# Plain 16-bit transposes of the attention outputs, and another table of scheduling settings

## The chip, the cores and the metric

The kernel runs on one core of a Trainium2 chip. The metric is the device time of one execution in microseconds (us). The engines are called by their short names: PE is the matrix engine, DVE the vector engine, ACT the activation engine, POOL the general engine, and SP the engine that issues most of the DMAs.

## The reference

Two attentions over the same x are mixed by a gate. S is 2048 tokens, D is 640, and there are 32 heads of 20.

```python
x = A_x
g = sigmoid((x * gate_w).sum(-1, keepdims=True))
a = full softmax attention: softmax(q k^T * 20**-0.5) v, 32 heads, then @ A_wo
b = sliding attention over 8 keys per query, 2 tokens apart (masked below 0), then @ B_wo
return g * a + (1 - g) * b
```

The full attention has 32 heads x 2048 x 2048 scores. Their exponentials are the bulk of the work.

## The kernel before

**Units and tiles.** The scores of four heads and 512 queries form a group: there are 32 groups (`NG`), 8 sets of heads for each of 4 chunks of queries. A group is cut into 64 units: 128 keys x 512 queries of one head, and so 2048 units in all. One unit is one 512-column matmul of `qk` (line 1515) into one bank of the PSUM. A tile is what one ACT instruction works on: two or three units side by side in one of two score buffers of 1536 columns (`exp`, line 1538, writes `ebuf`).

**Units that go to DVE.** The third bank of a score buffer can hold instead a unit that "rides" on the tile: DVE makes 16-bit integers of it, which read as bf16 are an approximate exponential (line 1528, `uD`). For each four such units (a quad) DVE also makes three shifted copies (line 797, `eD`), and POOL scales a copy of v for these (line 789, `vS`). PE then adds `uD` and the three `eD` to the output with one matmul each. So a unit is worth one ACT share of a tile, or one `uD`, three quarters of an `eD`, and four matmuls in place of one.

**PV and norm.** `pv` (line 1583) accumulates v^T p of a whole group in one bank, `obank`. When a group is done, `gen_norm` moves it out: DVE transposes it in blocks of 32 x 32 (line 758, `oTt`), takes reciprocals (line 762), POOL multiplies by gate and reciprocal (lines 764 and 770; DVE for the last group), and DVE transposes the bf16 result back (line 772, `oN1`). In the kernel before, line 770 writes the tokens in an order such that the back-transpose can take two bf16 as one 32-bit element: 256 elements in place of 512. Tokens then lie interleaved in `oN1` and `oTd`, and `paired` gives every later matmul a strided view of them, 32 columns at a time (lines 557 and 1063).

**Side work.** Generators with priorities do the rest in the gaps: projections of q, k and v, the sliding attention (`gen_b`, `gen_bproj`), the output projection of a finished chunk (`gen_fold`), and for the last chunk all of that projection but its last head set (`gen_prefold`, `gen_prefold2`). `tail` adds that last set (line 1063), adds up (lines 1076, 1082, 1085), and sends the last four row blocks off, two by ACT's DMA queue and two by SP's (line 1090). Matmuls of `filler` (line 1604) have no use but to keep PE busy where it would wait.

**What sets the order.** `_Sched` has an assumed time for every operation and lays the program out one tile after the other. Eighteen settings steer the choices: how far ahead of PE a side operation may be placed, which priorities get a third bank, how idle DVE must be for a riding unit (`DWAIT`, `DIDLE`, `DIDLE2`), the load under which fillers are put in (`FILL`), and so on. `PLAN` is a table of them by tile number: at tile s the row of s, if there is one, replaces all eighteen.

Of the kernel before, what the change touches and what calls it, by code (L numbers as in the profile page):

```python
# [5 lines left out]
FP32 = mybir.dt.float32  # L6
# [44 lines left out]
    0: ((0.34, 0.64), 0.37, 6.3, 2.5, 0.51, -1.0, -0.1, 11.8, 4.5, 7.2, 0.52, 0.47, 4.4, 1.86, 0.0, 0.85, 2, 0.0),  # L51
    10: ((0.34, 0.64), 0.37, 6.3, 2.5, -0.17, -1.0, -0.1, 13.02, 4.5, 7.2, 0.52, 0.47, 4.4, 1.86, 0.0, 0.85, 2, 0.0),
    20: ((0.34, 0.64), 0.21, 6.3, 6.6, -0.17, -1.0, -0.1, 13.02, 4.5, 8.28, 0.52, 0.47, 4.4, 1.86, 0.0, 0.85, 2, 0.0),
    30: ((0.28, 0.52), 0.35, 2.5, 6.6, 0.49, -1.55, -0.55, 9.24, 6.7, 7.2, 0.53, 0.57, 4.23, 4.64, 0.02, 0.85, 2, 1),
    50: ((0.28, 0.52), 0.35, 2.5, 6.6, 0.49, -1.55, -0.55, 9.24, 6.7, 7.2, 0.25, 0.57, 4.23, 4.64, -0.13, 0.85, 2, 1),
    60: ((0.28, 0.52), 0.35, 2.5, 6.6, 0.49, -1.55, -0.55, 9.24, 6.7, 7.2, 0.53, 0.57, 4.23, 4.28, 0.16, 0.85, 2, 1),
    70: ((0.28, 0.52), 0.1, 2.5, 6.6, 0.49, 0.2, -0.55, 9.24, 6.7, 7.2, 0.5, 0.57, 4.23, 4.64, 0.02, 0.85, 2, 1),
    80: ((0.28, 0.52), 0.34, 2.5, 5.5, 0.49, -1.55, -0.62, 9.24, 7.0, 7.2, 0.53, 0.57, 4.55, 4.64, 0.02, 0.85, 2, 1),
    90: ((0.28, 0.52), 0.3, 2.5, 6.6, 0.49, -1.55, -0.55, 9.24, 6.7, 7.8, 0.5, 0.57, 4.23, 4.64, 0.02, 0.85, 2, 1),
    110: ((0.28, 0.52), 0.3, 2.5, 6.6, 0.49, -1.55, -0.55, 8.84, 6.7, 7.8, 0.5, 0.57, 4.23, 4.64, 0.02, 0.85, 2, 0),  # L60
    120: ((0.28, 0.52), 0.3, 5.5, 6.6, 0.49, -1.34, -0.55, 8.84, 6.7, 7.8, 0.5, 0.57, 4.23, 4.64, 0.05, 0.85, 2, 0),
    130: ((0.28, 0.52), 0.19, 5.5, 6.3, 0.49, -0.24, -0.53, 9.24, 6.7, 11.3, 0.53, 0.57, 4.23, 4.93, -0.13, 0.89, 2, -3),
    140: ((0.28, 0.52), 0.3, 2.5, 2.5, 0.87, -1.55, -0.55, 8.84, 6.7, 7.8, 0.5, 0.57, 3.8, 4.64, 0.02, 0.85, 2, 0),
    170: ((0.28, 0.52), 0.3, 2.5, 2.5, 0.87, -1.28, -0.55, 8.42, 6.7, 7.8, 0.5, 0.54, 3.8, 4.64, 0.02, 0.85, 2, 0),
    180: ((0.28, 0.52), 0.39, 6.6, 2.5, 0.87, -1.55, -0.65, 10.03, 6.7, 7.8, 0.5, 0.57, 3.8, 3.83, 0.02, 0.87, 2, -3),
    190: ((0.28, 0.52), 0.19, 2.5, 2.5, 0.7, -1.55, -0.55, 7.32, 6.7, 7.8, 0.5, 0.5, 3.8, 2.96, 0.02, 0.85, 2, -3),
    200: ((0.23, 0.54), 0.35, 2.5, 2.5, 0.87, -1.55, -0.55, 7.13, 6.7, 7.71, 0.5, 0.57, 3.46, 4.13, 0.02, 0.86, 2, -3),
    210: ((0.28, 0.52), 0.3, 2.5, 2.5, 0.9, -1.55, -0.6, 7.13, 6.7, 7.71, 0.5, 0.49, 3.46, 4.64, 0.02, 0.85, 2, -3),
    220: ((0.32, 0.54), 0.3, 2.5, 2.5, 1.16, -1.55, -0.6, 7.13, 6.7, 7.71, 0.5, 0.49, 3.46, 4.64, 0.02, 0.85, 2, -3),
    230: ((0.28, 0.52), 0.3, 2.5, 2.5, 0.9, -1.55, -0.6, 7.61, 6.7, 7.71, 0.5, 0.49, 3.46, 4.64, 0.02, 0.81, 2, -3),  # L70
    250: ((0.28, 0.52), 0.3, 2.5, 2.5, 0.9, -1.48, -0.27, 7.13, 4.5, 7.32, 0.5, 0.36, 3.46, 4.64, 0.02, 0.66, 2, -3),
    280: ((0.28, 0.52), 0.3, 2.5, 2.5, 0.9, -1.48, -0.27, 7.13, 4.5, 7.32, 0.5, 0.41, 3.46, 4.64, 0.02, 0.66, 2, -3),
    290: ((0.28, 0.52), 0.3, 2.5, 5.5, 0.9, -1.6, -0.6, 7.13, 6.7, 10.69, 0.5, 0.49, 3, 4.64, 0.02, 0.67, 2, -3),
    310: ((0.28, 0.52), 0.3, 2.5, 5.5, 0.9, -1.6, -0.6, 14.73, 6.7, 10.69, 0.5, 0.49, 5.63, 4.64, 0.02, 0.67, 2, -3),
    320: ((0.28, 0.52), 0.3, 2.5, 5.5, 1.26, -1.56, -0.6, 7.13, 6.7, 10.69, 0.5, 0.53, 3, 4.64, 0.02, 0.67, 2, -3),
    330: ((0.27, 0.53), 0.26, 2.5, 5.5, 0.58, -1.6, -0.6, 7.13, 4.5, 10.54, 0.5, 0.49, 3, 4.64, 0.11, 0.67, 2, -3),
    340: ((0.27, 0.53), 0.3, 2.5, 5.5, 0.9, -1.5, -0.6, 7.13, 7.0, 10.54, 0.41, 0.49, 3.17, 4.64, 0.2, 0.67, 2, -3),
    350: ((0.27, 0.53), 0.26, 1.0, 5.5, 0.58, -1.6, -0.6, 7.13, 4.5, 10.54, 0.5, 0.49, 3, 4.64, 0.02, 0.69, 1, -3),
    360: ((0.28, 0.52), 0.37, 2.5, 5.5, 1.26, -1.56, -0.6, 7.13, 6.7, 10.69, 0.5, 0.53, 5.91, 4.64, 0.02, 0.67, 2, -3),
    400: ((0.28, 0.52), 0.37, 2.5, 5.5, 1.26, -1.56, -0.6, 7.13, 4.5, 10.69, 0.5, 0.53, 5.91, 4.64, 0.02, 0.67, 2, -3),  # L80
    410: ((0.23, 0.54), 0.22, 2.5, 6.3, 1.26, -1.56, -0.6, 7.13, 6.7, 10.69, 0.5, 0.53, 5.35, 4.64, 0.02, 0.6, 2, -3),
    420: ((0.24, 0.49), 0.3, 2.5, 5.5, 1.26, -1.56, -0.59, 7.13, 6.7, 10.69, 0.5, 0.53, 6.0, 4.64, 0.02, 0.67, 2, -3),
    430: ((0.24, 0.49), 0.3, 2.5, 5.5, 1.26, -1.56, -0.59, 7.13, 6.7, 10.69, 0.51, 0.53, 6.0, 4.64, 0.02, 0.67, 2, -3),
    450: ((0.26, 0.56), 0.3, 2.5, 5.5, 1.26, -1.56, -0.59, 7.13, 6.7, 10.69, 0.5, 0.53, 6.0, 4.64, 0.02, 0.67, 2, 0),
    480: ((0.26, 0.56), 0.3, 2.5, 5.5, 1.26, -1.4, -0.59, 9.8, 6.7, 10.69, 0.5, 0.53, 6.0, 4.64, 0.02, 0.67, 2, 0),
    500: ((0.26, 0.56), 0.3, 2.5, 5.5, 1.26, -1.56, -0.59, 7.13, 6.7, 10.69, 0.5, 0.53, 6.0, 4.64, 0.02, 0.76, 2, -1.5),
    510: ((0.26, 0.56), 0.3, 2.5, 5.5, 1.26, -1.56, -0.09, 7.13, 6.7, 10.69, 0.5, 0.53, 6.0, 4.64, 0.02, 0.76, 2, -3),
    530: ((0.21, 0.59), 0.3, 2.5, 6.6, 1.26, -1.56, -0.43, 7.13, 6.7, 10.69, 0.5, 0.53, 6.0, 4.64, -0.23, 0.76, 2, -3),
    540: ((0.21, 0.58), 0.3, 6.6, 5.5, 1.26, -0.43, -0.09, 7.13, 6.7, 10.33, 0.5, 0.53, 6.0, 4.64, 0.08, 0.76, 2, -3),
    550: ((0.21, 0.59), 0.3, 2.5, 6.6, 1.26, -1.56, -0.43, 7.13, 6.7, 11.31, 0.49, 0.53, 6.0, 4.64, -0.36, 0.76, 2, -3),  # L90
    570: ((0.2, 0.61), 0.3, 2.5, 6.6, 1.26, -1.56, -0.43, 7.13, 6.7, 10.69, 0.5, 0.53, 6.0, 4.64, -0.23, 0.76, 2, -3),
    580: ((0.2, 0.56), 0.3, 2.5, 5.5, 1.26, -1.56, 0.15, 9.66, 6.7, 8.54, 0.49, 0.48, 6.0, 4.64, -0.36, 0.76, 2, -3),
    590: ((0.2, 0.56), 0.26, 2.5, 1.0, 1.26, -1.56, 0.15, 7.13, 6.7, 11.31, 0.49, 0.31, 6.0, 4.64, -0.36, 0.76, 2, -3),
    600: ((0.28, 0.45), 0.32, 2.5, 5.5, 1.26, -0.49, -0.43, 10.79, 5.5, 10.35, 0.57, 0.53, 6.0, 4.64, -0.33, 0.66, 2, -3),
    630: ((0.28, 0.45), 0.32, 2.5, 5.5, 0.96, -0.49, -0.43, 10.79, 5.5, 10.35, 0.65, 0.53, 6.0, 4.64, -0.33, 0.66, 2, -3),
    660: ((0.28, 0.45), 0.32, 2.5, 5.5, 0.96, -0.1, -0.27, 10.79, 5.5, 10.35, 0.65, 0.53, 6.0, 4.64, -0.33, 0.66, 2, -3),
    670: ((0.28, 0.5), 0.32, 2.5, 5.5, 1.11, -0.49, -0.43, 10.79, 6.2, 10.35, 0.65, 0.55, 6.5, 4.81, -0.39, 0.62, 2, -3),
    690: ((0.3, 0.64), 0.32, 2.5, 2.5, 0.49, -1.0, -0.1, 11.8, 5.5, 7.2, 0.52, 0.47, 4.4, 4.0, 0.0, 0.85, 2, 0.0),
    700: ((0.42, 0.48), 0.32, 6.3, 5.5, 0.76, -0.49, -0.43, 10.79, 5.5, 10.35, 0.65, 0.53, 6.0, 4.64, -0.33, 0.63, 2, -3),
# [220 lines left out]
def _build(ctx, nc, A_x, A_wqkv, A_wo, B_wqkv, B_wo, gate_w, out):  # L320
# [221 lines left out]
    def mm_group(b, mms, reads, cost, first=True, last=True, per=1):  # L542
# [3 lines left out]
        for i0 in range(0, n, per):  # L546
            i1 = min(n, i0 + per)
            yield ("pe", sum(cost[i0:i1]) if isinstance(cost, list) else cost * (i1 - i0), rdy)

            def fn(e, i0=i0, i1=i1):  # L550
                ins = None
                for i in range(i0, i1):
                    o, l, r = mms[i]
                    n_ = P if callable(l) else l.shape[-1]
                    for j in range(0, n_, 32):
                        k = min(j + 32, n_)
                        ins = e.matmul(o[j:k, :], l(j) if callable(l) else l[:, j:k], r, start=(first and i == 0),  # L557
                                       stop=(last and i == n - 1), skip_group_check=True)
                return ins

            c = sum(cost[i0:i1]) if isinstance(cost, list) else cost * (i1 - i0)
            if i0 == 0 and first:
                T("pe", c, fn, reads=reads, writes=[("side", b)], mode="col")
            else:
                T("pe", c, fn, reads=reads, accum=[("side", b)], mode="col")
# [190 lines left out]
    def gen_norm(g):  # L756
# [9 lines left out]

        ib = _ap(rcp, 0, [[4, 4], [2, 2], [1, 2], [0, 32]])
        oo = _ap(oN[0], 0, [[128, 4], [1, 2], [64, 2], [2, 32]])
        ii = _ap(oTt, 0, [[128, 4], [64, 2], [32, 2], [1, 32]])
# [1008 lines left out]
```

## Time and profile before

| What | Value |
|---|---|
| Median of three runs (lowest to highest) | 837.19 us (836.29 to 837.24) |
| The profiled execution: its own time | 837.19 us |
| The profiled execution: its span | 835.4 us |
| Granted PE clock, mean | 0.998 |
| Busy time in the span: PE, ACT, DVE, POOL | 789.3, 803.9, 683.7, 138.7 us |
| ACT tiles of 1024, 1536 and 512 columns | 479, 255, 1 |
| Riding units (`uD`), shifted copies (`eD`) | 324, 243 |

The span is the time from the first to the last instruction in the trace. The execution's own time is 1.8 us longer, and equals the median. Busy times are those of a single execution. A "wait" in the profile is idle time of an engine before an instruction, with what ended it.

### The profile page before, as it was taken

The numbers are of one execution on the slowest core, as the hardware profiler recorded it, in microseconds if no ns is written. First come the engines' busy times: TensorE is split into PE (matmuls) and PEld (weight loads), VectorE is DVE, ScalarE is ACT, GpSimd is POOL, SyncE is SP. The second block draws the span as 40 slices with busy tenths as digits, with TensorE's granted clock in tenths as the row PEclk, the third lists the DMA queues.
The fourth block names the chain that finished last, engine by engine and source line by source line (L and its number), as shares of the span: only waits on it lengthen the run. The fifth ranks groups of instructions, "written<-read, shape, count | busy, mean of one in ns | idle before, by whom it ended". The sixth has DMA issues, their size and how long they took to land.

```text
span 835.4 us, 29602 instructions
## 1 busy us (share of the span) xinstructions
PE 789.3 (94%) x12599; PEld 289.9 (35%) x12601; DVE 683.7 (82%) x1205; ACT 803.9 (96%) x767; POOL 138.7 (17%) x180
## 2 busy tenths in 40 slices
PE   8999999999999899989998999999999999998997
PEld 4333323334333332333233333333333333333223
DVE  7567888889888887978797988798898898887873
ACT  4999999999999999999999999999999999999994
POOL 5013013431111111011111011111102111101110
PEclk9999999999999999999999999999999999999999
DMA  9112112200111110011001011110011001101100
GB/s 313 30 37 44 33 25 45 73 13 19 29 37 29 29 30 20 7 42 32 20 18 41 18 20 29 36 42 9 5 39 30 10 20 25 38 6 31 32 6 34
DMA packets 45016, 29.15 MB, mean 35 GB/s; under 512 B 27204, under 2 KB 43684, under 8 KB 44884
## 3 DMA queue, kind: packets, MB, share of 16 engines
q1 hardware_dynamic: 44596, 26.92, 12.4%
q8 instruction: 100, 1.64, 0.8%
q10 hardware_dynamic: 288, 0.33, 0.1%
q14 instruction: 32, 0.26, 0.1%
HBM read 11.94 MB, written 2.62 MB: 17 GB/s over the span
## 4 chain that ended last, share of the span: by engine, by line
PE 54%; ACT 30%; issue 10%; DVE 5%; DVEq 0%; ACTq 0%
ACT ebuf L1538 30%; PE score L1515 17%; PE obank L1583 13%; PE side L557 13%; PE score L557 5%; PE obank L1604 2%; DVE uD L1528 1%; PE side L1604 1%; DVE eD L797 1%; PE obank L459 1%; PE score L1230 1%; PE side L885 1%; DVE stage L869 0%; PE score L1604 0%; DVE stage L970 0%
## 5 line engine op out<-in xcount | busy, mean ns | idle before, releaser
L1538 ACT ACTIVATE ebuf<-score 128x1024 bf16<-128x1024 f32 (+1 forms) x735 | 792.6, 1237 | 11.6 <-PE score L1515 9.7
L1515 PE MATMUL score<-qT,kT 32*128 32x512 bf16 x2048 | 291.9, 384 | 31.6 <-ACT ebuf L1538 20.6
L1528 DVE TENSOR_SCALAR uD<-score 128x512 int16<-128x512 f32 x324 | 217.2, 683 | 38.4 <-PE score L1515 36.1
L797 DVE TENSOR_SCALAR eD<-uD 128x2048 int16<-128x2048 int16 x243 | 168.1, 722 | 7.9 <-PE obank L1583 7.2
L1515 PEld LDWEIGHTS score<-qT,kT 32*128 32x128 bf16 x2048 | 75.1, 91 | 282.7 <-ACT ebuf L1538 137.6
L1583 PE MATMUL obank<-ebuf,vA 128*21 128x512 bf16 x1724 | 161.3, 385 | 2.2 <-ACT ebuf L1538 1.8
L789 POOL TENSOR_TENSOR vS<-vA,vw 128x252 bf16<-128x252 bf16 x81 | 61.0, 757 | 291.5 <-PE obank L1583 256.3
L557 PE MATMUL side<-xT,kvw 128*32 128x256 bf16 (+1 forms) x2530 | 103.0, 281 | 3.1 <-DVE qkvB L853 1.4
L1583 PE MATMUL obank<-eD,vS 128*21 128x512 bf16 x972 | 84.1, 382 | 0.0
L557 PEld LDWEIGHTS side<-xT,kvw 128*32 128x32 bf16 x2530 | 59.3, 96 | 37.9 <-issue 22.0
L764 POOL TENSOR_TENSOR rcp<-rcp,gA 128x16 f32<-128x16 f32 x31 | 11.3, 365 | 351.9 <-DVE rcp L762 351.9
L1583 PEld LDWEIGHTS obank<-ebuf,vA 128*21 128x21 bf16 x1724 | 38.6, 89 | 82.3 <-issue 69.5
L970 DVE TENSOR_TENSOR stage<-qkvB,repB 128x1280 bf16<-128x1280 bf16 x64 | 52.9, 856 | 0.7 <-DMA repB<-eB 0.7
L869 DVE TENSOR_TENSOR stage<-qkvB 128x1280 bf16<-128x1280 bf16 x64 | 51.4, 830 | 0.1
L853 DVE CAST qkvB<-side 128x512 bf16<-128x512 f32 (+1 forms) x72 | 41.9, 591 | 10.5 <-PE side L557 10.5
L557 PE MATMUL side<-stage,ident 128*32 128x512 bf16 (+1 forms) x736 | 47.4, 345 | 1.2 <-DVE uD L744 0.5
L1604 PE MATMUL obank<-xT,zero 128*32 128x512 bf16 x444 | 37.9, 385 | 0.0
L770 POOL TENSOR_TENSOR oN<-oTt,rcp 128x512 bf16<-128x512 f32 x31 | 33.0, 1065 | 2.4
L1583 PE MATMUL obank<-uD,vA 128*21 128x512 bf16 x324 | 31.7, 382 | 0.0
L758 DVE STREAM_TRANSPOSE oTt<-obank 128x512 f32<-128x512 f32 x32 | 22.7, 709 | 9.0 <-PE obank L1583 8.9
L1583 PEld LDWEIGHTS obank<-eD,vS 128*21 128x21 bf16 x972 | 24.0, 92 | 17.4 <-issue 4.1
L557 PE MATMUL side<-woA_d,oTd 128*32 128x128 bf16 (+1 forms) x580 | 28.8, 293 | 0.0
(173 smaller groups left out, 555.5 us busy)
## 6 DMA issues: line engine op xcount, KB each, us to landing
repB<-eB SPq DMA_DIRECT2D x128, 32.0 KB
WqP<-in_A_wqkv_dram SPq DMA_DIRECT2D x16, 160.0 KB
stage<-in_B_wqkv_dram SPq DMA_DIRECT2D x1, 2400.0 KB
oTd<-oN SPq DMA_DIRECT2D x108, 20.0 KB
qT<-dst SPq DMA_DIRECT2D x104, 20.0 KB
out_dram<-outsb SPq DMA_DIRECT2D x12, 160.0 KB
kvw<-in_A_wqkv_dram SPq DMA_DIRECT2D x2, 800.0 KB
oTd<-in_A_x_dram SPq DMA_DIRECT2D x2, 640.0 KB
```

The costliest lines, as they stand in the source:

```text
L557: ins = e.matmul(o[j:k, :], l(j) if callable(l) else l[:, j:k], r, start=(first and i == 0), stop=(last and i == n - 1), skip_group_check= ...
L770: T(en, c2, lambda e: e.tensor_tensor(oo, ii, ib, ALU.mult), reads=["rcp", "oTt"], writes=["oN0"])
L789: T("pool", 0.7, lambda e: e.tensor_tensor(vS[:, d % 2, :, :], _ap(vA, (kb * NQ + q) * 4 * DV, [[0, K - 1], [1, 4 * DV]]), _ap(vw, 0, [[1, ...
L797: T("dve", 0.11 + 0.1334 * n, lambda e, k=k, sl=sl: e.tensor_scalar(eD[:, sl % NS, 0:512 * n].bitcast(I16), uD[d % 2][:, 0:512 * n].bitcas ...
L853: t = TB(dvc(n * TOK), lambda e, o=o, i=i: e.tensor_copy(o, i), reads=[("side", b)], writes=[key])
L869: TB(dvc(CN * TOK, 2), lambda e, w=w, ks=ks: e.tensor_tensor(prodB(w), qB[:, :, :], ks, ALU.mult), reads=["qB", "kB"], writes=[("prod", w) ...
L970: TB(dvc(CN * TOK, 2), lambda e, w=w, vs=vs, rr=rr: e.tensor_tensor(prodB(w), vs, rr, ALU.mult), reads=["vB", ("repB", w4 % NR)], writes=[ ...
L1515: ins = e.matmul(o, kT[32 * j:32 * j + 32, q, kb * P:(kb + 1) * P], qT[g % NQT][32 * j:32 * j + 32, :], start=True, stop=True)
L1528: t = T("dve", 0.69, lambda e: e.tensor_scalar(uD[d % 2][:, 512 * i:512 * (i + 1)].bitcast(I16), side[x], UOFF, 0.0, op0=ALU.add, op1=ALU. ...
L1538: exps[s] = T("act", actc(512 * n), lambda e: e.activation(ebuf[s % NE][:, 0:512 * n], score[s % 2][:, 0:512 * n], ACTF.Exp, scale=LN2 / S ...
L1583: ins = e.matmul(obank[32 * j:32 * j + DV, :], v, src, start=(kb == 0), stop=(last and k >= len(lst) - 4), skip_group_check=True)
L1604: ins = e.matmul(o[32 * j:32 * j + 32, :], w[:, 32 * j:32 * j + 32] if best else w[:, :], xT[:, 0, 0:512], start=bool(best), stop=bool(bes ...
```

## The change

The words that came with the change speak of the head (the last K block in a free score bank, the first Q in the output bank) and of the last output rows leaving by two DMA queues. The diff does not touch these places: `kbank` and its callers, and the four output DMAs on ACT's and SP's queues, read the same in both files. What the diff does is two things.

First, the paired transpose goes. Line 770 writes the tokens in plain order, line 772 transposes 512 bf16 elements in place of 256 32-bit ones, `paired` is gone, and the projections take plain slices. The matmuls of `tail` go back from four of 32 columns each to one of 128.

Second, all rows of `PLAN` are replaced. The table before has 49 rows at multiples of 10, the table after 46 at multiples of 8; the first and last rows are shown here.

```diff
 PLAN = {
-    0: ((0.34, 0.64), 0.37, 6.3, 2.5, 0.51, -1.0, -0.1, 11.8, 4.5, 7.2, 0.52, 0.47, 4.4, 1.86, 0.0, 0.85, 2, 0.0),
...
-    700: ((0.42, 0.48), 0.32, 6.3, 5.5, 0.76, -0.49, -0.43, 10.79, 5.5, 10.35, 0.65, 0.53, 6.0, 4.64, -0.33, 0.63, 2, -3),
+    0: ((0.3, 0.64), 0.32, 2.5, 2.5, 0.49, -1.0, -0.16, 11.8, 7.0, 8.62, 0.51, 0.47, 4.21, 4.0, 0.0, 0.85, 2, 0.0),
+    8: ((0.25, 0.64), 0.27, 2.5, 2.5, 0.49, -1.0, -0.27, 12.76, 7.0, 7.2, 0.52, 0.47, 4.4, 4.0, 0.0, 0.85, 3, 0.0),
...
+    704: ((0.41, 0.79), 0.35, 2.5, 2.5, 0.75, -1.6, 0.19, 14.48, 7.0, 9.44, 0.43, 0.36, 3.33, 3.58, 0.2, 0.69, 2, -3),
 }
...
-                    n_ = P if callable(l) else l.shape[-1]
-                    for j in range(0, n_, 32):
-                        k = min(j + 32, n_)
-                        ins = e.matmul(o[j:k, :], l(j) if callable(l) else l[:, j:k], r, start=(first and i == 0),
+                    for j in range(0, l.shape[-1], 32):
+                        k = min(j + 32, l.shape[-1])
+                        ins = e.matmul(o[j:k, :], l[:, j:k], r, start=(first and i == 0),
                                        stop=(last and i == n - 1), skip_group_check=True)
...
-        ib = _ap(rcp, 0, [[4, 4], [2, 2], [1, 2], [0, 32]])
-        oo = _ap(oN[0], 0, [[128, 4], [1, 2], [64, 2], [2, 32]])
-        ii = _ap(oTt, 0, [[128, 4], [64, 2], [32, 2], [1, 32]])
+        ib = _ap(rcp, 0, [[1, 16], [0, 32]])
+        oo = oN[0][:, :].rearrange("p (b c) -> p b c", c=32)
+        ii = _ap(oTt, 0, [[32, 16], [1, 32]])
         T(en, c2, lambda e: e.tensor_tensor(oo, ii, ib, ALU.mult), reads=["rcp", "oTt"], writes=["oN0"])
         yield ("dve", DVE_AHEAD, max(sch.ready("oN0"), sch.free("oN1")))
-        T("dve", dvc(256), lambda e: e.transpose(oN[1][:, :].bitcast(FP32), oN[0][:, :].bitcast(FP32)), reads=["oN0"], writes=["oN1"])
+        T("dve", dvc(512), lambda e: e.transpose(oN[1][:, :], oN[0][:, :]), reads=["oN0"], writes=["oN1"])
...
-    def paired(of, blk):
-        at = lambda j: blk * P + 2 * (j % 64) + j // 64
-        return lambda j: of(slice(at(j), at(j) + 63, 2))
...
-            return [(o, paired(lambda c: oN[1][:, c], blk), woA_l[:, c0:c1])]
+            return [(o, oN[1][:, tok], woA_l[:, c0:c1])]
...
-        return mms + [(o, paired(lambda c, f=f: oTd[0:rows[f], (QCN - 1) % 2, f, c], blk), woA_d[0:rows[f], f, c0:c1])
-                      for f in range(CN)]
+        return mms + [(o, oTd[0:rows[f], (QCN - 1) % 2, f, tok], woA_d[0:rows[f], f, c0:c1]) for f in range(CN)]
...
-                    for j in range(0, P, 32):
-                        ins = e.matmul(o[j:j + 32, :], l(j), r, start=not accum, stop=True, skip_group_check=True)
+                    ins = e.matmul(o, l, r, start=not accum, stop=True, skip_group_check=True)
                 return ins
-            T("pe", sum(0.215 if o.shape[-1] > 128 else 0.06 for o, _, _ in lst), fn, reads=rd, mode="col",
+            T("pe", sum(0.215 if o.shape[-1] > 128 else 0.06 for o, _, _ in lst), fn, reads=rd,
               **({"accum": [key]} if accum else {"writes": [key]}))
...
-                (o, paired(lambda c, f=f: oTd[:, qc % 2, f, c], blk), woA_d[:, f, c0:c1]) for f in range(CN)]
+                (o, oTd[:, qc % 2, f, tok], woA_d[:, f, c0:c1]) for f in range(CN)]
```

Because `_Sched` lays out the whole program anew from the changed durations and settings, almost every tile of the changed kernel differs in what it holds and in what stands beside it. Counted over both instruction streams:

| Instructions | Before | After |
|---|---|---|
| ACT `exp` of 1536, 1024, 512 columns | 255, 479, 1 | 293, 428, 1 |
| Units for ACT, riding units | 1724, 324 | 1736, 312 |
| `eD` copies on DVE, `vS` on POOL | 243, 81 | 234, 78 |
| PV matmuls (from `ebuf`, `uD`, `eD`) | 3020 | 2984 |
| Back-transposes on DVE | 32 of 128x256 (32-bit) | 32 of 128x512 (bf16) |
| Filler matmuls | 748 | 844 |

## The prediction

> **What bounds the kernel now.** I read the page's busy time and chain first, then ACT's busy time by stretch.
>
> ```profile
> PE 789.3 (94%) x12599; PEld 289.9 (35%) x12601; DVE 683.7 (82%) x1205; ACT 803.9 (96%) x767; POOL 138.7 (17%) x180
> ...
> PE 54%; ACT 30%; issue 10%; DVE 5%; DVEq 0%; ACTq 0%
> ```
>
> ```profile
> core 0: us, ACT busy (x), PEclk, DMA share, GB/s
> 0.00:19.60 19.60, 8.11 (x10) 1.00 0.95 307
> 19.60:823.85 804.25, 794.66 (x755) 1.00 0.11 28
> 823.85:836.00 12.15, 1.08 (x2) 0.96 0.15 56
> ```
>
> The chain gives PE 54%, which misleads: PE's busy time holds 748 filler matmuls, and chain steps between PE and ACT change hands at every tile. The stretches are clearer. From the first `exp` (19.62 us) to the end of the last (823.82 us) ACT is busy 794.66 of 804.25 us. It idles 9.6 us in all. So the time is a head of 19.6, ACT's work, 9.6 of gaps, a tail of 11.6 (to 835.4), and 1.8 us outside the span, which makes 837.19, the median itself.
>
> The groups of instructions with shapes apart, and the waits, give ACT's prices and what its gaps are:
>
> ```profile
> L1538 ACT ACTIVATE ebuf<-score 128x1024 bf16<-128x1024 f32 x479 | 463.4, 1082 | 6.4 <-PE score L1515 5.0
> L1538 ACT ACTIVATE ebuf<-score 128x1536 bf16<-128x1536 f32 x255 | 359.2, 1530 | 5.1 <-PE score L1515 4.4 <-ACT ebuf L1538 0.2
> ...
> L1528 DVE TENSOR_SCALAR uD<-score 128x512 int16<-128x512 f32 x324 | 217.2, 683 | 38.4 <-PE score L1515 36.1
> ```
>
> ```profile
> ACT ebuf L1538 <- PE score L1515: 9.7, 24, 2.1
> ```
>
> The reader is to see that ACT waits for scores alone, 24 times, 2.1 us of it before the first tile.
>
> **Part 1, ACT's work.** The two means differ by 448 ns for 512 columns, which is the price of a unit. The page has 792.6 us for all 735 tiles (neighbours overlap, so the two groups' busy times must not be added). 1724 units x 0.448 = 772.4, so 20.2 us or 27.5 ns stay for each tile. After: 1736 units x 0.448 + 722 tiles x 0.0275 = 777.7 + 19.9 = 797.6 us. That is **+5.0 us** (12 units more, 13 tiles fewer), on the path, since ACT has nothing to hide it under. If the share per tile were 60 ns, the slope would fall and the term be 4.4. I keep 5.0.
>
> **Part 2, DVE.** The 32-bit transposes of 512 elements (line 758) take 22.7/32 = 0.709 us, those of 256 (line 772) 13.9/32 = 0.434. The bf16 one of 512 isn't in the trace. Lower bound: 0.434, if bf16 goes two at a time. Upper bound: 0.709, one element at a time. I take 0.709, the nearest row in count of elements: +0.275 x 32 = +8.8 us. Off go 12 `uD` at 217.2/324 = 0.670 (-8.0) and 9 `eD` at 168.1/243 = 0.692 (-6.2). DVE's sum is -5.4 us (-14.2 at the lower bound). DVE is busy 664 of the 804 us between first and last `exp`, so neither is on the path as a sum. It counts only where DVE runs behind for a moment and PE waits for a bank. The DMAs of `oTd` on SP's queue start up to 0.275 us later behind each transpose; their readers are folds that wait for a whole chunk, so nothing.
>
> The page "VectorE: DVE Perf Modes", section "Mode 2×_1P — pack two bf16 into one 32-bit read", has a rule against my 0.709: packed 16-bit elements are read two per cycle. By that rule the transpose would stay at 0.434 and the sum of DVE be -14.2; no row here shows a 16-bit transpose.
>
> **Part 3, PE and POOL.** 36 PV matmuls fewer, four side by side; 80 of 512 columns at the end take 4.76 us (below), 59.5 ns each, so -2.1 us; the 96 more fillers are +5.7 us, placed where the planner sees PE idle. Plain slices as weights: loads from the strided `oTd` take 96 ns in the mean and so do those from `woBp`, `oB` without a stride, so nothing. POOL makes three `vS` fewer (-2.3 us). Line 770 without the interleaved write lies between DVE's 0.751 for the same operation and the slowest here, 1.476, against 1.05 now; DVE waited for it 4.6 us in all, so I take nothing, with bounds of -2 and +2 on DVE, off the path.
>
> **Part 4, the tail.** The chain's last pieces in order of time:
>
> ```profile
> 823.22 0.61 ACT ebuf L1538
> 823.82 0.04 issue
> 823.87 0.40 PE obank L1583 x4
> 824.26 1.12 PE side L557 x56
> 825.38 4.76 PE score L557 x80
> 830.14 1.23 PE score L1063 x32
> ```
>
> The tail is bound by PE: 56 matmuls of 128 columns and 80 of 512 stand on PE's queue between the last PV and line 1063, 5.88 us, although `oN1` was ready at 826.87. In the changed stream 8 PV matmuls are last (0.21 more), and 72 of 512 columns stand behind them: 72 x 59.5 ns = 4.28 us. That is -5.88 + 0.21 + 4.28 = **-1.4 us**. DVE's chain ends 0.21 + 0.275 later, at 827.4 on the old clock, still 1.4 us ahead of PE's 828.8, so this back-transpose costs nothing. If that cover were gone, it would cost 0.3. The rest of the projection ran earlier, under `exp`. Line 1063 has eight matmuls for 32; four of 128 and four of 512 columns take as long side by side as alone (20 of 128 columns full width take 1.12 us, five of 512 1.08), so nothing.
>
> **Part 5, the gaps.** The 9.6 us are 2.2 in the head (0.97, 0.33, 0.92), where the first tiles of both streams are nearly alike, and 7.4 later, in pieces of 0.15 to 0.64. What an entirely different layout makes of them no row prices. For less: DVE has 5.4 us less to do, and the worst place now (452.7 to 460.3 us, 1.5 us of gaps) shows PE waiting for DVE. For more: PE stretches between two score matmuls with over 1.2 us of other work number 28 for 15. Those of before mostly cost nothing (1.6 us of work near 663 us, no gap). I take 0, with -7.4 and +5.9 (13 more stretches at 0.45, as the larger gaps) as bounds.
>
> Sum: 837.19 + 5.0 - 1.4 + 0 = **840.8 us**.
>
> **Rivals.** *The gaps close (faster).* The mechanism is DVE's backlog: if the freed 5.4 us lie where `uD` evictions hold a bank up, the gaps after 60 us go. Full price -7.4: 833.4 us. It decides once gaps fall by over 5.3 us, which makes 835.5. For it: PE's waits for DVE before the gaps at 452 to 458 us. Against: 5.4 of 684 us is little, and it would need more than two thirds of these gaps to go.
>
> *The clock falls more often (much slower).* The windows around the worst gaps:
>
> ```profile
> 455.00:457.00 2.00, 1.48 (x18) 0.56 (x19) 2.00 (x5) 2.00 (x3) 0.00 (x1) 0.79 0.20 53
> 457.00:459.00 2.00, 2.00 (x23) 0.54 (x19) 0.60 (x1) 1.36 (x2) 1.92 (x3) 0.50 0.13 29
> 459.00:461.00 2.00, 2.00 (x50) 1.03 (x42) 0.00 (x0) 1.63 (x2) 0.37 (x1) 0.86 0.04 8
> ```
>
> The columns are PE, PEld, DVE, ACT, POOL busy, granted clock, DMA. The clock was at half once, about 456.3 to 459.7 us, and two gaps of 0.64 and 0.37 lie in it. One such fall is 1.0 us; five more, with the stretches' 5.9, give 840.8 + 5 + 5.9 = 851.7 us. For it: fillers are set by other `FILL` values, between 0.6 and 0.87. Against: 96 more fillers. The page "TensorE: Matmul & The Clock Gate", section "Part 1: The HAM clock gate", has the half clock follow an idle window of some 3.4 us. The trace disagrees in part: in 452.9 to 456.3 us PE was busy 2.23 of 3.40 us. By the page's rule alone there would be no falls in the middle at all, and this rival would keep only its 5.9.
>
> *No change.* The head and the output queues, of which the words of the change speak, are alike in both files, so from these alone the time would be 837.2. As a whole it needs gaps smaller by 1.9 to 5.3 us, to eat up the 3.6 of parts 1 and 4.
>
> **How the numbers follow.** A measurement of this kernel can tell about 0.2%, 1.7 us, from no change: 835.5 to 838.9. The forecast (gaps of -1.9 to +5.9 against now: 838.9 to 846.7) gets 0.64, more gaps or clock falls 0.12, no change 0.13, closed gaps 0.11. Slower is 0.64 + 0.12. The range reaches from 836.0 (gaps -4.8) to 846.5 (+5.7), which leaves out 0.08 below and 0.12 above.
>
> **What would show it.** Right: L1538 busy near 797.6 us with 722 tiles, ACT's idle time between first and last `exp` at 7 to 15 us, the last `exp` to line 1052 (old 1063) 5.0 us in place of 6.3, line 767's transpose near 0.7 us, DVE's busy time near 678 us. Wrong: a mean of a 1536 tile off 1.53, ACT idle under 4.5 us (faster) or above 15.5 (clock in the rows at 0.5 again and again), or a tail that DVE ends.

## The result, and the profile after

The changed kernel took 843.16 us in the median of four executions, against 837.22 us for the kernel before beside it. One of the four, the profiled one, had the PE clock at 0.654 from end to end and took 1021 us; the other three took 842.17 to 843.34 us, 842.98 in the median, and these give a ratio of 1.0069, with a 95% interval of 1.0049 to 1.0089. The change makes the kernel slower by 0.7%. The profile after is read from another run of the unchanged file, called `after_again` below. Its profiled execution took 842.05 us with a span of 840.3 us.

The busy times of the page:

```profile
PE 786.3 (94%) x12637; PEld 291.9 (35%) x12637; DVE 674.7 (80%) x1184; ACT 809.3 (96%) x754; POOL 138.4 (16%) x177
```

Against before, ACT has 5.4 us more, DVE 9.0 us less, and PE 3.0 us less. ACT's busy time by stretch, cut at the start of the first `exp` and the end of the last:

```profile
core 0: us, ACT busy (x), PEclk, DMA share, GB/s
0.00:18.84 18.84, 8.12 (x11) 1.00 0.96 302
18.84:828.99 810.15, 800.14 (x742) 1.00 0.12 28
828.99:840.30 11.31, 1.09 (x3) 0.89 0.17 61
```

The middle stretch grew from 804.20 to 810.15 us, and ACT's busy time in it from 794.66 to 800.14 us. ACT idles 10.0 us in it, against 9.5. So nearly all of the growth lies in ACT's busy time, and the gaps give none of it back. The groups with shapes apart (busy us, mean ns, idle time before them):

```profile
L1527 ACT ACTIVATE ebuf<-score 128x1024 bf16<-128x1024 f32 x428 | 413.8, 1059 | 9.0 <-PE score L1504 7.5 <-PE side L553 0.3
L1527 ACT ACTIVATE ebuf<-score 128x1536 bf16<-128x1536 f32 x293 | 408.4, 1500 | 3.1 <-PE score L1504 2.6
...
L1517 DVE TENSOR_SCALAR uD<-score 128x512 int16<-128x512 f32 x312 | 209.3, 685 | 53.4 <-PE score L1504 50.4 <-PE obank L1572 0.4
```

Line 1527 is the old 1538, and 1517 the old 1528. The shape of 1536 columns has 293 tiles for 255. Both shapes' means fell (1530 to 1500 ns, 1082 to 1059), because neighbours overlap by other amounts (the single durations add up to 116 us more than the engine's busy time before, and to 96 us more after); all 722 tiles together keep the engine busy for 797.6 us. What ACT waits for, by the waits:

```profile
ACT ebuf L1527 <- PE score L1504: 10.1, 20, 2.2
```

It is the same wait as before, 20 times in place of 24. The chain's last pieces in order of time show the end:

```profile
829.04 0.61 PE obank L1572 x8
829.66 1.84 PE score L553 x32
831.49 2.38 PE side L553 x40
833.88 0.55 PE score L1052 x5
```

Eight PV matmuls stand last, then 72 matmuls of 512 columns in 1.84 + 2.38 = 4.22 us. Line 1052 starts 833.88 - 828.99 = 4.89 us after the last `exp` ends by this view, and its first instruction in the trace, a weight load, 4.82 us after.

The account from before to after, in the spans of the two profiled executions: head -0.8 (first `exp` at 18.84 in place of 19.62; two other runs with the layout after have 19.6, and `frozen_plain`, with the layout before, has 18.84, so this is no effect of the change), ACT's busy time +5.5, gaps +0.5, last `exp` to line 1052 -1.4, and from DVE's last addition to the end of the span +1.2 (3.9 us in place of 2.7). The sum is +5.0, and 840.3 - 835.4 is 4.9.

### The profile page after: what moved, and what is told of

Same layout as the page of the kernel before. It is cut to its first block, busy times and chain, and to the rows that moved or that the text cites. A ratio compares the mean times of both kernels' runs of the same rounds, so it can differ in the third digit from the quotient of the medians.

```text
span 1019.2 us, 29615 instructions
## 1 busy us (share of the span) xinstructions
PE 995.7 (98%) x12634; PEld 326.9 (32%) x12637; DVE 683.1 (67%) x1184; ACT 853.0 (84%) x754; POOL 136.8 (13%) x177
## 4 chain that ended last, share of the span: by engine, by line
PE 92%; ACT 5%; DVE 2%; issue 1%; DVEq 0%; ACTq 0%
PE side L553 26%; PE score L1504 25%; PE obank L1572 24%; PE score L553 6%; ACT ebuf L1527 4%; PE obank L1593 3%; PE score L1593 2%; PE side L1593 1%; PE side L880 1%; PE score L1219 1%; PE obank L456 1%; DVE uD L1517 0%; DVE qkvB L848 0%; DVE eD L792 0%; PE obank L1242 0%
## 5 line engine op out<-in xcount | busy, mean ns | idle before, releaser
L1527 ACT ACTIVATE ebuf<-score 128x1536 bf16<-128x1536 f32 (+1 forms) x722 | 840.3, 1197 | 139.9 <-PE score L1504 130.6
L1504 PE MATMUL score<-qT,kT 32*128 32x512 bf16 x2048 | 325.7, 439 | 12.1 <-ACT ebuf L1527 8.3
L1572 PE MATMUL obank<-ebuf,vA 128*21 128x512 bf16 x1736 | 189.6, 455 | 0.4 <-DVE oTt L754 0.2
L553 PE MATMUL side<-xT,kvw 128*32 128x256 bf16 (+1 forms) x2560 | 138.6, 348 | 1.1 <-DVE qkvB L848 0.5
L1572 PE MATMUL obank<-eD,vS 128*21 128x512 bf16 x936 | 110.7, 507 | 0.0
L553 PEld LDWEIGHTS side<-xT,kvw 128*32 128x32 bf16 x2560 | 72.9, 111 | 50.3 <-issue 29.8
L553 PE MATMUL side<-stage,ident 128*32 128x512 bf16 (+1 forms) x768 | 64.3, 444 | 0.4 <-DVE qbnd L687 0.2
L1593 PE MATMUL obank<-xT,zero 128*32 128x512 bf16 x440 | 48.3, 484 | 0.0
L553 PE MATMUL side<-woA_d,oTd 128*32 128x512 bf16 (+3 forms) x560 | 38.7, 378 | 0.0
L553 PE MATMUL side<-woBp,oB 128*32 128x512 bf16 (+1 forms) x560 | 36.6, 375 | 0.0
```

Of the source, the lines that this page charges most:

```text
L553: ins = e.matmul(o[j:k, :], l[:, j:k], r, start=(first and i == 0), stop=(last and i == n - 1), skip_group_check=True)
L1504: ins = e.matmul(o, kT[32 * j:32 * j + 32, q, kb * P:(kb + 1) * P], qT[g % NQT][32 * j:32 * j + 32, :], start=True, stop=True)
L1527: exps[s] = T("act", actc(512 * n), lambda e: e.activation(ebuf[s % NE][:, 0:512 * n], score[s % 2][:, 0:512 * n], ACTF.Exp, scale=LN2 / S ...
L1572: ins = e.matmul(obank[32 * j:32 * j + DV, :], v, src, start=(kb == 0), stop=(last and k >= len(lst) - 4), skip_group_check=True)
L1593: ins = e.matmul(o[32 * j:32 * j + 32, :], w[:, 32 * j:32 * j + 32] if best else w[:, :], xT[:, 0, 0:512], start=bool(best), stop=bool(bes ...
```

## The experiments

Medians stand beside those of the kernel before on the same chip, with the ratio and its 95% interval.

### The file again, and the two halves of the change with the layout kept

`after_again` is the changed file as it is. The other two take the halves of the change apart, so that the planner lays out exactly the same program: each is told the durations that belong to its table, whichever transposes it really has. `frozen_plain` is the file after with the table before and with plain transposes. `frozen_paired` is the file before with the table after and with paired transposes.

```diff
 frozen_plain, from the file after, with the PLAN of before:
-        T("dve", dvc(512), lambda e: e.transpose(oN[1][:, :], oN[0][:, :]), reads=["oN0"], writes=["oN1"])
+        T("dve", dvc(256), lambda e: e.transpose(oN[1][:, :], oN[0][:, :]), reads=["oN0"], writes=["oN1"])
...
-            T("pe", sum(0.215 if o.shape[-1] > 128 else 0.06 for o, _, _ in lst), fn, reads=rd,
+            T("pe", sum(0.215 if o.shape[-1] > 128 else 0.06 for o, _, _ in lst), fn, reads=rd, mode="col",
 frozen_paired, from the file before, with the PLAN of after: the same two edits, the other way round
```

> The changed kernel as it is, for a profile at full clock. It takes about 5.8 us more than before, and the prediction's terms give 3.6. Theory A (ACT's work decides): L1527 is busy 797.6 us in 722 tiles, the tail from the last exp to line 1052 is 5.0 us, and the 2.2 us that are missing stand in ACT's gaps, which grow from 9.6 to about 11.8 us. Theory B (a mis-sized tail): ACT's gaps stay at 9.6 us and the tail stays at 6.3 to 7 us. Theory C (the clock falls more often): rows at a clock of 0.5 in two or more places away from the ends, each with about 1 us of gaps.

> The layout of before, instruction for instruction, but with the plain transposes: the planner is told the old durations. Only the 32 back-transposes (and their layout of tokens, the slices and the eight tail matmuls) differ. Theory A: DVE hides 8.8 us more of transposes but for moments of backlog, so 837.2 to 838.2 us. Theory D (the transposes themselves are on the path): at least half of the 5.8 us of the whole change, 840 us or more. A transpose of 512 bf16 elements takes 0.709 us by the prediction, 0.434 if two elements go at a time.

> The layout of the changed kernel, instruction for instruction, but with the paired transposes (and the 32 tail matmuls of 32 columns): the planner is told the new durations. Theory A: 842 to 843 us, the same as the changed kernel within 1 us, since ACT has the same tiles. Theory D: 840 us or less.

Measured: `after_again` 842.22 against 836.68 us, 1.0066 (1.0051 to 1.0081). Theory A's 797.6 us and its shorter tail came true, but the gaps grew by 0.5 us and not by 2.2. `frozen_plain` 838.58 us (ten executions, 835.97 to 841.38), 1.002 (1.0002 to 1.0037); the profiled one took 836.54 us, with 9.55 us of gaps and the same tail as before. `frozen_paired` 842.77 us, 1.0082 (1.0065 to 1.0099).

The layout decides. With the layout of after, no difference between the two transposes can be told (842.77 and 842.22). With the layout of before the slower transpose costs 0.02 to 0.37%, or up to some 3 us: the median is 1.9 us up, a little more than the 837.2 to 838.2 us that were expected. The profiled execution is one of the fastest of the ten, so no trace shows where the others lost this. Yet the slower transpose is real, as the group of the kernel before and then that of `frozen_plain` show:

```profile
L772 DVE STREAM_TRANSPOSE oN<-oN 128x256 f32<-128x256 f32 x32 | 13.9, 436 | 4.8 <-POOL oN L770 4.6
L770 DVE STREAM_TRANSPOSE oN<-oN 128x512 bf16<-128x512 bf16 x32 | 22.5, 703 | 4.8 <-POOL oN L768 4.6
```

It is 703 ns for 436, so 8.6 us of DVE's time come in, most of it beside other work.

### One half at a time, laid out anew

`transpose_only` is the file after with the table before; `plan_only` is the file before with the table after. Here the planner knows the true durations, and lays out a program that neither of the two kernels has.

> The code of after with the table of before, laid out anew. By the instruction stream ACT has 1740 units in 758 tiles, 800.4 us or 7.8 us more than before, and 160 matmuls of 128 columns stand before the 80 of 512 columns behind the last PV, which makes the tail some 2 us longer. Theory A with gaps unchanged: 837.2 + 7.8 + 2 = 847 us. Theory E (the new settings make the gaps, and the old ones don't): 845 us or less, with gaps under 9.6 us.

> The code of before (paired transposes) with the table of after, laid out anew. By the instruction stream ACT has 1756 units in 724 tiles: 806.6 us, 14.0 more than before; behind the last PV stand 60 matmuls of 512 columns, 3.57 us for 5.96. Theory A with gaps as before: 836.7 + 14.0 - 2.4 = 848.3 us. Theory E (each table fits the durations it came with, and a foreign layout gets more gaps): 852 us or more, with ACT's gaps above 13 us.

Measured: `transpose_only` 866.23 us, 1.0356 (1.0341 to 1.0371). `plan_only` 859.43 us, 1.0267 (1.0252 to 1.0282). Both are misses of the sums by 11 to 19 us; for `plan_only` the expectation's second theory, 852 us or more with over 13 us of gaps, came true. ACT's part was forecast well: by 448 ns a unit and 27.5 ns a tile `plan_only` should have 806.6 us in `exp` and has 806.9, and `transpose_only` should have 800.4 and has 802.5. What was missed are gaps (18.3 and 14.0 us of ACT's idle time between first and last `exp`, for 9.5) and, in `transpose_only`, the tail. ACT's waits there:

```profile
ACT stage L1074 <- PE side L1055: 22.6, 1, 22.6
ACT ebuf L1530 <- PE score L1507: 14.5, 32, 2.1
```

One wait of 22.6 us stands behind the last `exp`: the projection of the last chunk is nearly all still to be done. The expectation had looked only at the last rows of the stream. In these two cases, then, a table of settings served only with the durations that it came with. With the other ones it gives a program that is some 23 or 30 us slower than the kernel before, and each half of the change alone is worse than both together.

### Some of ACT's work away, some added

If the 12 units more on ACT are the cause, taking them away should give their time back, and added work should cost its own time. `after_minus12` leaves the exponential of 12 units out (the third unit of every 24th wide tile; PV reads what the buffer held). `before_plus24` adds 24 ACT instructions of 256 columns, whose output nobody reads, to the kernel before. Both layouts are otherwise unchanged.

```diff
 after_minus12, in exp():
+        m = 2 if n == 3 and cnt[3] % 24 == 18 else n
...
-            ebuf[s % NE][:, 0:512 * n], score[s % 2][:, 0:512 * n], ACTF.Exp, scale=LN2 / STEP),
+            ebuf[s % NE][:, 0:512 * m], score[s % 2][:, 0:512 * m], ACTF.Exp, scale=LN2 / STEP),
 before_plus24, ahead of the exp of each tile with n == 2 and cnt[2] % 20 == 10:
+            e.activation(spare[:, :], score[s % 2][:, 0:256], ACTF.Exp, scale=LN2 / STEP)
```

> The changed kernel with its layout kept, but in 12 tiles spread over the run ACT leaves out the third 512 columns: 12 units' exponentials are not computed, so that ACT has 1724 units as before. PE, DVE, POOL and the DMAs are untouched. Theory A (ACT's work is the path nearly everywhere): 12 x 0.448 = 5.4 us less than the changed kernel's 842.2, so 836.8 us, the time of before. Theory F (PE, busy 94%, is as much the bound as ACT): 2 us less or nothing.

> The kernel before with its layout kept, but ahead of 24 tiles ACT computes 256 columns once more into a spare buffer. Nothing else is added or waits for it. By the price of a unit that is 24 x (0.224 + 0.0275) = 6.0 us of ACT work. Theory A: 836.7 + 6.0 = 842.7 us. Theory F: 839 us or less, since ACT's additions fall into time that it would have waited for PE.

Measured: `before_plus24` 841.45 us, 1.0062 (1.0043 to 1.0081). `after_minus12` 841.24 us against 836.78, 1.0071 (1.0045 to 1.0097), which is not told apart from the file after. The middle stretch of each, ACT alone, first `before_plus24`:

```profile
18.88:828.75 809.87, 800.73 (x779) 1.00 0.12 28
```

```profile
19.59:828.14 808.55, 796.30 (x742) 1.00 0.11 28
```

Added work comes through: ACT's busy time is 6.07 us up on the kernel before and the stretch 5.67 (the median is 4.7 us up). Work taken away mostly does not: ACT's busy time is 3.84 us down on the file after (5.4 were expected for the 12 units), but its idle time is up from 10.0 to 12.25, and the stretch is only 1.6 us shorter. So ACT alone is not the bound: with the 1724 units of before, the layout of after still takes 4.5 us more than the kernel before.

The two traces have the same tiles in the same order, so they can be laid side by side. At six of the 12 places the eighth tile behind the shortened one starts just as it would have without it, within 0.01 us; one place keeps the whole 0.42 us, and the other five 0.11 to 0.30. One of the six in `after_minus12`, first ACT, where the shortened tile is the last of the four, and then the busy times (PE, PEld, DVE, ACT, POOL, clock, DMA) from its start to that of the third tile behind it:

```profile
685.56 4.65 ACT L1530 ACTIVATE ebuf<-score 128x1024 bf16<-128x1024 f32 x4
690.46 7.92 ACT L1530 ACTIVATE ebuf<-score 128x1536 bf16<-128x1536 f32 x7 [0.25 <-PE score L1505]
```

```profile
689.13:692.84 3.71, 3.71 (x77) 1.63 (x69) 1.76 (x3) 3.44 (x4) 0.61 (x1) 1.00 0.10 27
```

ACT now waits for scores, where the file after has no wait, and PE is busy all the time. Over the six such stretches together PE is busy 23.30 of 23.69 us, with four filler matmuls in all. What holds the scores back there is thus PE's other matmuls (scores, PV and side work) in the order that the planner wrote, and neither a wait of PE nor the fillers. This is a reading of one trace, and it says nothing of the other places.

### The fillers made thin

Would less work on PE, at the same places, let the shorter `exp` through? `minus12_thin` is `after_minus12` with filler matmuls of 16 columns in place of 512, so that PE has less to do at the same places.

```diff
-                ins = e.matmul(o[32 * j:32 * j + 32, :], w[:, 32 * j:32 * j + 32] if best else w[:, :], xT[:, 0, 0:512], start=bool(best),
+                n = 16
+                ins = e.matmul(o[32 * j:32 * j + 32, 0:n], w[:, 32 * j:32 * j + 32] if best else w[:, :], xT[:, 0, 0:n], start=bool(best),
```

> The kernel that leaves out the third 512 columns of 12 tiles on ACT, with its layout kept, but every filler matmul has 16 columns in place of 512. The fillers' results are used nowhere. Theory F1 (PE's queue, with fillers placed for ACT's planned times, is as tight as ACT): without the fillers' 844 x 0.0535 = 45 us PE keeps ahead, and the 5.4 us of ACT come through, 837 to 838 us, unless the clock falls. Theory F2 (the gaps are waits for DVE and for the order of work, not the fillers): 841 us as with them. Clock theory (PE is kept at full clock by the fillers): stretches at a clock of 0.5 in many places, and 845 us or more.

Measured: 851.04 us, 1.0178 (1.0143 to 1.0214), with a mean clock of 0.96, as the clock theory had it. The windows of one of its falls (PE, PEld, DVE, ACT, POOL busy, granted clock, DMA):

```profile
758.00:760.00 2.00, 1.60 (x21) 0.47 (x18) 1.80 (x5) 2.00 (x3) 0.00 (x0) 1.00 0.00 0
760.00:762.00 2.00, 1.36 (x22) 0.46 (x22) 1.86 (x7) 2.00 (x3) 0.00 (x0) 1.00 0.03 8
762.00:764.00 2.00, 1.33 (x11) 0.32 (x9) 1.96 (x4) 2.00 (x3) 1.64 (x3) 0.86 0.00 0
764.00:766.00 2.00, 1.39 (x38) 0.65 (x38) 0.80 (x2) 2.00 (x3) 0.64 (x1) 0.50 0.06 16
```

PE was busy 1.36 and 1.33 of 2 us, and then had half the clock. The clock fell so in nine places, and ACT's idle time went to 20.8 us. In `after_minus12` it had fallen once, with a mean of 0.997. The experiment answers another question than the one asked: the fillers hold the clock up. What PE's load alone does to the time stays open.

### The tail of after in the layout of before

The tail of after was 1.4 us shorter, so its last row of settings was put into the table before, at a place where it leaves the number of ACT's units nearly as it was.

```diff
-    700: ((0.42, 0.48), 0.32, 6.3, 5.5, 0.76, -0.49, -0.43, 10.79, 5.5, 10.35, 0.65, 0.53, 6.0, 4.64, -0.33, 0.63, 2, -3),
+    695: ((0.41, 0.79), 0.35, 2.5, 2.5, 0.75, -1.6, 0.19, 14.48, 7.0, 9.44, 0.43, 0.36, 3.33, 3.58, 0.2, 0.69, 2, -3),
```

> The kernel before with one row of its table changed: the last row of the table of after, at tile 695 in place of row 700. ACT keeps its 1724 units (734 tiles), and behind the last PV stand 60 matmuls of 512 columns in place of 80 and 56 of 128: 3.57 us for 5.96. Theory A with the tail as predicted (PE bound, until DVE's chain of about 3.1 us takes over): 2.3 us faster, 834.4 us. If the tail's gain is taken back by a later landing of the last rows, as it seems in the changed kernel (6.5 us from line 1052 to the end in place of 5.3): 835.6 us.

Measured: 836.56 us, 1.0005 (0.9993 to 1.0018), where 834.4 or 835.6 were expected. From the last `exp` to the tail's first matmul there are 4.17 us in place of 6.25, as meant. But ACT idles 12.35 us in the middle stretch instead of 9.54. Of these 2.8 us, 1.7 lie behind 810 us, and the timeline of ACT's last tiles shows where (start, us, then in brackets the idle time before):

```profile
812.19 2.79 ACT L1538 ACTIVATE ebuf<-score 128x1536 bf16<-128x1536 f32 x2 [0.56 <-PE score L1515]
815.65 6.26 ACT L1538 ACTIVATE ebuf<-score 128x1024 bf16<-128x1024 f32 x5 [0.67 <-PE score L1515]
822.22 1.45 ACT L1538 ACTIVATE ebuf<-score 128x1536 bf16<-128x1536 f32 x1 [0.32 <-PE score L1515]
```

A fourth wait of 0.41 us follows. Before, the waits behind 810 us were 0.26 and 0.18 us. The projection that no longer stands behind the last `exp` stands before it, on the same PE, and the last scores come later. No version that was run beats the kernel before.

### The last microsecond

The time from DVE's last addition to the end of the span was 2.7 us before and 3.9 after, with the same four output DMAs. Of the queues in the last 5 us one differs, that of instruction fetches (packets, MB, share), first the file after:

```profile
q14 instruction: 2, 0.02, 0.8%
```

The other runs with the number of DVE instructions of after have two such packets too: `frozen_paired`, `after_minus12` and `after_pool8` end 3.9 us after the last addition, `minus12_thin` 3.1. The kernel before and the other runs have one, and end 2.7 to 2.8 us after it. Whose block is the second? With the instructions that the page does not count as busy, DVE has 1344 in the trace of the file after and 1362 before. `after_dve18` adds 18 tiny memsets on DVE in the head, and `after_pool8` adds 8 on POOL.

```diff
 after_dve18:
+    for i in range(18):
+        T("dve", 0.0, lambda e: e.memset(spare[:, :], 0.0), writes=["spare"])
 after_pool8:
+    for i in range(8):
+        T("pool", 0.1, lambda e: e.memset(spare[:, :], 0.0), writes=["spare"])
```

> The changed kernel with 18 tiny memsets more on DVE in the head, where it waits for the transposes of x; DVE then has as many instructions as in the kernel before. Theory H (the second packet at the end is DVE's): one packet, 2.7 us from DVE's last addition to the end, 841.1 us. If it isn't: 3.9 us and 842.2 us.

> The changed kernel with eight tiny memsets more on POOL in the head, where POOL is idle afterwards; nothing else moves. POOL then has as many instructions as in the kernel before. In the changed kernel's layouts two packets of instructions (8 KB each) are fetched while the last output rows are under way, and the end comes 3.9 us after DVE's last addition; in the other layouts it is one packet and 2.7 to 2.8 us. Theory G (the second packet is POOL's, and depends on how many instructions it has): one packet, 2.7 us, and 1.1 us off the whole, 841.1 us. If it isn't POOL's: 3.9 us and 842.2 us, as before.

Measured: with POOL's eight there are two packets still and 3.86 us to the end. With DVE's 18 there is one, and 2.72 us. The queue in the last 5 us of `after_dve18`, and SP's wait for its output DMA in that run and then in the file after:

```profile
q14 instruction: 1, 0.01, 0.7%
```

```profile
SPq L287 <- DMA out_dram<-stage: 0.9, 1, 0.9
```

```profile
SPq L287 <- DMA out_dram<-stage: 2.0, 1, 2.0
```

Each of these rests on one profiled execution, but they agree with the second block being DVE's, and with it the wait for the output DMA is 1.1 us longer here. Why `minus12_thin` loses only 0.4 us by its second packet stays open. The medians do not confirm that this brings 1.1 us: `after_dve18` took 842.52 us, 1.0075 (1.0053 to 1.0098), like the file after, where 841.1 were expected. Its profiled execution, the slowest of its four, had 12.7 us of gaps, 2.7 more than `after_again`, with the clock at half around 382 to 392 us. `after_pool8` took 847.12 us, 1.0114 (1.0079 to 1.015), its executions between 841.7 and 848.01, where 842.2 were expected; its profiled one was the fastest, so its traces do not show what the others lost.

## Why the prediction was right

**ACT's work: right in size, half right in reason.** The forecast for line 1527 was 797.6 us, and 797.6 was measured. That the two agree to a tenth is luck. By the same prices the other layouts were off by 0.3 to 2.1 us, and in `after_minus12` each of the 12 shortened tiles is 423 to 428 ns shorter than in the file after, where the price of a unit was 448; with 427 ns the prediction's own sum leaves 77 ns for each tile and gives +4.1 us. The mean of a 1536 tile went from 1.53 to 1.50 us, which the prediction had named as a sign of being wrong; it was an ill-chosen sign, since the mean moves with the overlap of neighbours, while the busy time of all tiles together came out as forecast. That added work costs nearly its whole time is what `before_plus24` shows (5.67 of 6.07 us). That ACT "has nothing to hide it under" was read as ACT being the only bound, and that was too much: `after_minus12` got back about 1 us in the median, where the removed `exp` work was worth 3.8. So the 12 units alone do not make the kernel slower: at six of the 12 places looked at, PE's own work was just as long, and the prediction has no term for that. That the time came out right all the same is in part luck. The other ACT instructions add 0.5 us, as they overlap less with `exp` than before (2.5 us of busy time beside it, for 2.1); no term stood for that.

**DVE: right.** The transpose took 705 ns in place of 709:

```profile
L767 DVE STREAM_TRANSPOSE oN<-oN 128x512 bf16<-128x512 bf16 x32 | 22.6, 705 | 14.5 <-POOL oN L765 14.4
```

The Trainium skill, "VectorE: DVE Perf Modes", section "Mode 2×_1P — pack two bf16 into one 32-bit read", describes a mode in which packed 16-bit elements are read two per cycle. This transpose got nothing of it: 512 bf16 elements take as long as 512 of 32 bits from the PSUM (710 ns), and 256 pairs as 32-bit elements take 436. DVE's busy time is 674.7 us for a forecast of about 678. In the layout of after, `frozen_paired` shows no gain from the faster transpose, so none of it is seen on the path; in the layout of before the cost of 0.2 to 3.1 us stands against a forecast of nothing.

**POOL: the wait was outside its bounds.** Line 765 (the old 770) took 1060 ns, in its bounds and next to the 1065 of before. But DVE waited for it 14.4 us in place of 4.6, where at most 2 more were allowed for. It comes from the layout and not from the plain write: `frozen_paired`, with the interleaved write, has 14.5, and `frozen_plain` has 4.6. No run takes the wait away with this layout kept, so that it is off the path is not shown.

**The tail up to line 1052: right.** 4.82 us from the last `exp` to the tail's first matmul for a forecast of 5.0, and 6.25 before: -1.4. The 72 matmuls took 4.22 us for 4.28.

**The gaps: right within the bounds.** 10.0 us for 9.6, inside 7 to 15. The clock fell twice in place of once, around 380 to 384 and at 756 to 759 us. The rows of the first:

```profile
378.00:380.00 2.00, 1.37 (x11) 0.30 (x8) 1.93 (x5) 2.00 (x3) 0.00 (x0) 1.00 0.00 0
380.00:382.00 2.00, 1.96 (x43) 0.89 (x42) 1.45 (x3) 2.00 (x4) 0.32 (x2) 0.60 0.06 16
382.00:384.00 2.00, 1.86 (x22) 0.57 (x23) 1.38 (x3) 2.00 (x4) 1.52 (x2) 0.55 0.19 50
```

0.59 and 0.43 us of gaps lie beside the two, so the forecast's 1.0 us a fall was high. That there are two is not an effect of the change: `frozen_paired` and `after_pool8`, with the same layout, have one fall each, and without the first one the gap there is 0.15 us. The rivals with closed gaps and with many falls did not come.

**The missing 2 us.** The time is 2.4 us above the forecast's 840.8. By the profiled execution of `after_again`, 1.2 us are the end: "The tail" stopped at line 1063 and took the rest as it was, and the rest grew, it seems by DVE's block of instructions, though the medians of `after_dve18` do not confirm it. 0.5 are the other ACT instructions and 0.5 the gaps. In that execution a head that was 0.8 shorter hides part of this.

## What to carry to other kernels

Where one engine is busy for 99% of a stretch, added work on it cost nearly its full time here, but removed work mostly did not come back: a second engine was packed to nearly the same length. Taking work out shows this; a share of busy time does not. In a program that is laid out from assumed durations, settings and durations belong together, so take the halves of a change apart with the layout frozen before reading their effects; laid out anew, each half alone was some 23 to 30 us slower here, which neither shows with the layout kept. A tail ends with the last transfer to land, and not with the last instruction that computes.

## What the runs showed of the hardware that was not expected

- With one more block of instructions fetched in the last 5 us, the output DMA of SP's queue was waited for 2.0 us in place of 0.9 (1.2 in `minus12_thin`). 18 DVE instructions in the head, 800 us earlier, decided whether there is one, by one profiled execution each.
- Matmuls without a use, but of full width, kept the clock here. With 16 columns in place of 512 the clock fell nine times for once, in the case shown after two windows of 2 us in which PE was busy for two thirds. The Trainium skill, "TensorE: Matmul & The Clock Gate", section "Part 1: The HAM clock gate", has the half clock follow an idle window; in these rows PE had work in the windows ahead of the fall, and the share of work below which the clock falls is not known from them.
- A transpose of 512 bf16 elements takes 705 ns and one of 256 pairs 436, for the same bytes.
